# A third group of the first product as seven quarter products, with a new table of places

## The chip, the cores and the metric

The kernel runs on one core of a Trainium2 chip. The metric is the device time of one execution in microseconds; lower is better. The engines are named as in the profile: PE (TensorE, matrix products; PEld is its loading of weights), DVE (VectorE), ACT (ScalarE), POOL (GpSimd) and SP (SyncE); the last two only start transfers here, but for a tiny copy by which POOL waits.

## The reference

Eight batches of eight heads of normalised linear attention, then two matrix products with a leaky ReLU between them:

```python
kv = einsum('bhsd,bhse->bhde', k, v)            # 64 x 64 per head
o = einsum('bhsd,bhde->bhse', q, kv)            # 576 x 64 per head
x = o / sqrt(mean(o * o, -1) + 1e-6) * g_norm   # then 4608 tokens x 512
h = x @ w_in                                    # 4608 x 2048, "first product"
g = maximum(h, 0) + alpha * minimum(h, 0)
out = g @ w_out                                 # 4608 x 512, "second product"
```

Inputs and the output are float32. The kernel computes in float16 with float32 sums.

## The kernel before

The 4608 tokens are worked through in nine blocks (w = 0 to 8) of 512 tokens. A block needs the attention of its tokens (made while the block before it is in the products), the first product, and the second one, which runs into the next block. Blocks 0 and 1 are written out by hand. From block 2 on (line 1443 on) the work is a list of steps with a key, what it needs, and a function that records the instructions.

**The steps**, by the names that the text uses (block and number behind them):

- `M` (put_tile, L1513; m1_mm, L643): one of 16 tiles of 128 features of the first product, 4 matmuls of 128x512. The first of a block is parted in `Ma` (3 of 4 token tiles, L676) and the rest. `r` is ACT's ReLU of the negated tile (m1_neg, L652), `s` DVE's combine into g (m1_sum, L658).
- `f` (put_fast, L1464; m1_prod, L1254): the 16 tiles are four groups s = 0 to 3 of four tiles. A group can instead be made as a 2 x 2 block product by Strassen's scheme in Winograd's form: seven products of quarters, each 4 matmuls of 128x256. They stand in the order 1, 5, 6, 2, 7, 4, 3 of needs; products 1, 6, 7 and 4 add up in one PSUM bank Y. ACT copies that bank's state three times: `seed` (into bank X, L1270), `u2` and `u3` (L1273), and the next product may only add to Y when the copy is done: f6 after seed, f7 after u2, f4 after u3. DVE adds `c22` and `c12` (L1276), and ReLU (L1314) and combine (L1321) follow for the quarters 11, 12, 21, 22 (`r11`, `s11` and so on; a combine of a quarter is two instructions of 128x256).
- `t` (x_sum, L1233): four sums of quarters of x for these products, on DVE. `a` (a_sum, L1215): four sums of quarters of w_in for a group s, made once on DVE in block 2 and kept in a stage buffer of q, k or v that has become free.
- `p` (prod_mm, L862): a quarter of one of the seven products of the second product, 4 matmuls of 128x256, in the order 1, 2, 6, 7, 4, 5, 3 of products; its banks are read by the `y` steps (y_read, L929): `p1`, `seed`, `u2`, `u3`, `c11`, `c21` on ACT, `c22` and `c12` on DVE. `S` are its sums on DVE (s_pair, L806). `st` stores a quarter of the block's output (by POOL, `c12` by SP).
- `kv` and `kvc` (L1339, L1352): kv of a batch on PE, its copy on ACT. `R` (rows_mm, L508): the attention of two token tiles on PE; kv and the R steps of block 4 on use one PSUM buffer in turn. `q2`, `q3` (rows_sq, L584): squares and sums of a tile on ACT, 16 instructions; `rs` (L594) the reciprocal root on ACT; `n` (rows_norm, L610) the norm on DVE; `x` (x_move, L622) the transposing transfer into x, issued by SP.
- `ld` (put_load, L1705): a load of q, k or v, issued by POOL behind a copy of one element (gate, L1404) of the g that was recorded last; `q` (dma_t, L402): the transpose of a part of q, issued by SP.

**The order.** A table AT holds a number, a place, for each name. Prefixes of a name tell of block 2 (b), earlier (o), late ones (l) and block 8 (e); all other blocks share one entry, moved by 27.0 a block (LOOP). in_order takes, of the steps whose needs are recorded and whose buffer is to be had, the one with the smallest place:

```python
return (w - 2) * LOOP + AT[name], name
...
s = min((s for s in todo if usable(s)), key=lambda s: place(s[0])[0] + 1e-6 * rank[s[0]])
```

The order of recording is the order of each engine's queue. So the table decides what waits behind what on PE, ACT, DVE, POOL and SP; the steps from block 4 to block 7 stand in the same order in each block.

M1_FROM (L1200) says from which block on a group is made by quarter products; it is groups 2 and 3 from block 3 on. Four PSUM banks (h1, h2, m0, m1) go round among the tiles and the groups: a tile takes one, a group three (Y, V, X).

Of the kernel before, what the change touches and what calls it, by code (L numbers as in the profile page):

```python
# [17 lines left out]
def kernel(  # L18
# [1178 lines left out]
    h_turn[0] = 2  # L1197
    h_tags[0] = ("h1", "h0", "h2")

    M1_FROM = {2: 3, 3: 3}  # L1200
    HD = NC // 2
    spare, xsums, m1s = {}, {}, {}
    SPARE = {1: "q", 2: "k", 3: "v"}
# [556 lines left out]
    for w in range(1, NW):  # L1760
# [2 lines left out]

    LOOP = 27.0
    AT = {
# [67 lines left out]
    }  # L1833

    def place(key):

        what, w, *x = key
        if what == "f":
# [88 lines left out]
```

## Time and profile before

| | |
|---|---|
| median of 3 runs | 271.57 us (271.28 to 271.68) |
| the profiled execution | 271.5 us; span from first to last instruction 269.7 us |
| granted PE clock | 1.000 |
| transfers | 35.61 MB, mean 132 GB/s |
| PE, 128x512 of the first product (L643) | x348, 379 ns each |
| PE, 128x256 of the second product (L897) | x880, 273 ns each |
| PE, 128x256 of quarter products (L1254) | x336, 273 ns each |
| DVE, combine 128x512 (L658) | x96, 741 ns each |
| DVE, combine 128x256 (L1321) | x96, 474 to 479 ns each |
| ACT, ReLU of a tile (L652) | x96, 596 ns each |

The durations of one engine's instructions overlap: a matmul or a vector operation begins before the last one has ended. What an instruction costs its engine in a full queue is the time from its start to the next start, which the timeline of the engine gives. In the timeline a line holds a run of equal instructions: start, time until the last of them ended, engine, line, operation, what it writes from what, shapes, how many, and in brackets the idle time before it with what ended it.

### The profile page before, as it was taken

The page shows a single profiled execution, that of the slowest core. Times are in us where ns is not written, and L with a number is a line of the kernel's source. Part 1 is how long each engine was busy: PE and PEld are TensorE (multiplying, and loading weights), DVE is VectorE, ACT ScalarE, POOL GpSimd, SP SyncE. Part 2 cuts the span into 40 slices and gives each one's busy share as a digit, 9 for nine tenths or more (in the row PEclk, how much of TensorE's full clock was granted, in tenths as well). Part 3 has the DMA queues.
Part 4 walks back from the last instruction along what each step waited for, and adds up shares of the span by engine and source line. Part 5 has one row for each costly group of instructions (what it writes and reads, how often), then busy time and mean ns, then how long its engine had stood idle before and what let it go on. Part 6 is the DMA issues. An engine that isn't in the chain of part 4 may idle for free.

```text
span 269.7 us, 6668 instructions
## 1 busy us (share of the span) xinstructions
PE 262.0 (97%) x2430; PEld 182.4 (68%) x2430; DVE 225.8 (84%) x434; ACT 193.6 (72%) x686; POOL 94.6 (35%) x158
## 2 busy tenths in 40 slices
PE   7899999999999989999999999999999999999995
PEld 2454444456556756886688768876886688678884
DVE  7459727998987868988899889988998999978963
ACT  3567475786479789779977997799779974757410
POOL 8863453513530295470366043904130003001200
PEclk9999999999999999999999999999999999999999
DMA  7999999998998699999979989999664023100313
GB/s 151 193 201 202 197 197 193 174 197 113 173 188 122 77 136 169 171 183 145 148 88 165 191 115 85 122 192 144 93 123 113 1 41 118 41 0 2 131 66 118
DMA packets 91573, 35.61 MB, mean 132 GB/s; under 512 B 62980, under 2 KB 89748, under 8 KB 91540
## 3 DMA queue, kind: packets, MB, share of 16 engines
q0 software_dynamic: 57872, 23.83, 71.1%
q1 hardware_dynamic: 32628, 10.34, 22.4%
q10 hardware_dynamic: 1040, 1.02, 1.2%
q8 instruction: 19, 0.31, 0.5%
q14 instruction: 14, 0.11, 0.2%
HBM read 36.71 MB, written 9.44 MB: 171 GB/s over the span
## 4 chain that ended last, share of the span: by engine, by line
PE 76%; DMA 14%; ACT 4%; issue 2%; POOL 2%; DVE 1%; POOLq 0%; ACTq 0%
PE h_ps L643 20%; PE yY L897 15%; PE yX L897 9%; PE yZ L897 8%; PE mY L1254 8%; DMA w_out_sb<-in_moe_w_out_dram 5%; PE mV L1254 4%; DMA qst<-in_q_dram 4%; PE y L688 4%; DMA w_in_sb<-in_moe_w_in_dram 4%; ACT sq_sb L584 2%; PE h_ps L676 2%; PE mX L1254 2%; DMA qt_sb<-qst 2%; PE or_ps L521 1%
## 5 line engine op out<-in xcount | busy, mean ns | idle before, releaser
L643 PE MATMUL h_ps<-xt,w_in_sb 128*128 128x512 f16 x348 | 83.3, 379 | 0.0
L658 DVE SCALAR_TENSOR_TENSOR gt<-m_sb,beta_sb,h_ps 128x512 f16<-128x512 f32 x96 | 67.1, 741 | 4.7 <-ACT m_sb L652 4.0
L652 ACT ACTIVATE m_sb<-h_ps 128x512 f32<-128x512 f32 x96 | 54.7, 596 | 16.1 <-PE h_ps L643 12.9
L643 PEld LDWEIGHTS <-w_in_sb 128*128 128x128 f16 x348 | 33.0, 98 | 31.9 <-issue 0.4
L897 PEld LDWEIGHTS <-s 128*128 128x128 f16 x496 | 48.0, 98 | 8.7 <-DVE s L815 0.2
L897 PEld LDWEIGHTS <-gt 128*128 128x128 f16 x384 | 37.5, 98 | 8.2
L1404 POOL COPY gate_sb<-gt 1x1 f16<-1x1 f16 x39 | 11.9, 305 | 85.0 <-DVE gt L658 49.2
L584 ACT ACTIVATE sq_sb<-or_ps 128x64 f16<-128x64 f32 x192 | 39.6, 277 | 0.0
L584 ACT ACTIVATION_READ_ACCUMULATOR sq_sb<-or_ps 128x1 f32 x192 | 39.4, 264 | 0.0
L700 POOL DMA_DIRECT2D out_dram<-y_sb x32 | 20.5, 643 | 52.2 <-ACT y_sb L946 44.3
L897 PE MATMUL yX<-w_out_sb,gt 128*128 128x256 f16 x256 | 34.6, 273 | 0.0
L897 PE MATMUL yY<-wsum,s 128*128 128x256 f16 x256 | 32.3, 273 | 0.0
L610 DVE TENSOR_TENSOR x_rows<-or_ps,rstd_r 128x512 f16<-128x512 f32 x27 | 17.4, 686 | 11.4 <-ACT rstd_r L594 11.3
L1321 DVE SCALAR_TENSOR_TENSOR gt<-m_sb,beta_sb,mh 128x256 f16<-128x256 f32 x48 | 20.5, 479 | 1.3 <-ACT m_sb L1314 1.2
L1314 ACT ACTIVATE m_sb<-mh 128x512 f32<-128x512 f32 x24 | 15.1, 629 | 6.3 <-DVE mh L1276 6.3
L208 POOL DMA_DIRECT2D qst<-in_q_dram x20 | 17.9, 898 | 2.6 <-issue 2.2
L1273 ACT COPY mu<-mY 128x512 f32<-128x512 f32 x24 | 14.1, 589 | 4.9 <-PE mY L1254 4.4
L1276 DVE TENSOR_TENSOR mh<-mV,mu 128x512 f32<-128x512 f32 x24 | 16.4, 685 | 0.6 <-ACT mu L1273 0.4
L688 PE MATMUL y<-w_out_sb,gt 128*128 128x512 f16 x64 | 16.3, 379 | 0.4 <-DMA w_out_sb<-in_moe_w_out_dram 0.4
L897 PE MATMUL yZ<-wsum,s 128*128 128x256 f16 x120 | 16.2, 273 | 0.0
L897 PE MATMUL yY<-wsum,gt 128*128 128x256 f16 x128 | 15.4, 273 | 0.0
L1254 PEld LDWEIGHTS <-w_in_sb 128*128 128x128 f16 x144 | 14.1, 98 | 1.6
(147 smaller groups left out, 416.1 us busy)
## 6 DMA issues: line engine op xcount, KB each, us to landing
out_dram<-y_sb POOLq DMA_DIRECT2D x16, 256.0 KB, 3.2
kst<-in_k_dram POOLq DMA_DIRECT2D x7, 512.0 KB, 7.0
vst<-in_v_dram POOLq DMA_DIRECT2D x6, 512.0 KB, 8.8
qst<-in_q_dram POOLq DMA_DIRECT2D x20, 128.0 KB, 5.1
w_out_sb<-in_moe_w_out_dram POOLq DMA_DIRECT2D x8, 256.0 KB, 11.3
out_dram<-y_sb SPq DMA_DIRECT2D x5, 256.0 KB, 2.3
w_in_sb<-in_moe_w_in_dram POOLq DMA_DIRECT2D x2, 512.0 KB, 10.5
qst<-in_q_dram POOLq DMA_DIRECT2D x2, 512.0 KB, 12.3
```

The costliest lines, as they stand in the source:

```text
L208: nc.gpsimd.dma_start(out=stages[b, "q"][:, t, :, :], in_=srcs["q"][b, :, t * P : (t + 1) * P, :].rearrange("h p d -> p h d"),)
L584: nc.scalar.activation(out=sq[:, half, j], in_=o_ps[:, half, j], func=AF.Square, accum_out=ssq[:, half, j : j + 1],)
L610: nc.vector.tensor_tensor(out=xr[:].rearrange("p j h d -> p h j d"), in0=o_ps, in1=rstd[:].unsqueeze(3).to_broadcast([P, 2, NPAIR, D]), op ...
L643: nc.tensor.matmul(out=h_ps[:], lhsT=w_in_blk(c, g), rhs=xts[w][:, c, :], start=(c == 0), stop=(c == NC - 1),)
L652: nc.scalar.activation(out=neg[w, g][:], in_=h_ps[:], func=AF.Relu, scale=-1.0)
L658: nc.vector.scalar_tensor_tensor(out=gts[w, i][:, r, :], in0=neg.pop((w, g))[:], scalar=beta_sb[:, g : g + 1], in1=h_ps[:], op0=ALU.mult, ...
L688: nc.tensor.matmul(out=y[:], lhsT=gt_cols(w, g, a * P, (a + 1) * P), rhs=w_out_blk(g), start=(n == 1), stop=(n == NF),)
L700: engs[store_turn[0] % len(engs)].dma_start(out=dst, in_=src)
L897: nc.tensor.matmul(out=bank, lhsT=lhs, rhs=rhs, start=fresh, stop=(c == NK - 1), skip_group_check=True,)
L1254: nc.tensor.matmul(out=t[bank][:, r, :], lhsT=lhs[:, c, r * P : (r + 1) * P], rhs=rhs[:, c, :], start=(fresh and c == r == 0), stop=(c == ...
L1276: nc.vector.tensor_add(out=h_tile(t, what)[:, :, HW:W], in0=src[:], in1=u[:])
L1321: nc.vector.scalar_tensor_tensor(out=gts[w, i][:, r, cols], in0=m, scalar=beta_sb[:, g : g + 1], in1=h, op0=ALU.mult, op1=ALU.add,)
```

## The change

Two places of the kernel function change. Group s = 1 of the first product is made by seven quarter products from block 4 on, beside groups 2 and 3. So in blocks 4 to 8 four tiles M4 to M7 with their ReLUs and combines go, and the steps f11 to f17, seed, u2, u3, c22, c12 and the ReLUs and combines of four quarters come, and four sums a11 to a14 of w_in in block 2, kept in the second stage buffer of q. And all numbers of the table AT are new, with entries for the new steps, so that the order of every engine changes from block 2 on.

```diff
-    M1_FROM = {2: 3, 3: 3}
+    M1_FROM = {1: 4, 2: 3, 3: 3}
...
     LOOP = 27.0
     AT = {
-        "eyu3": -53629.57, "eyc21": -52723.24, "f2r11": -8398.49, "br7": -7586.48, "byu2": -7581.06,
...
+        "lkvc": -18398.72, "lq22": -18387.22, "lq23": -18384.30, "lq32": -18384.10, "r1": -18371.94,
...
+        "M0": 54.03, "M2": 54.03, "M1": 54.50, "M3": 54.81, "f11": 55.20, "bM12": 55.29, "ep23": 55.45,
...
+        "S30": 60.41, "f16": 60.63, "f21": 61.35, "M7": 61.86, "M5": 61.89, "f17": 62.03, "bM13": 62.09,
+        "f12": 62.19, "f15": 62.22, "f1s11": 62.90, "f14": 63.11, "f13": 63.25, "f1s22": 64.19, "f2c22": 64.26,
...
     }
```

The recorded order of PE for a whole block, before and after (block 5; a step with no block number belongs to it, and p4 is the second product of block 4):

```
before: M0 M2 p4:10 p4:11 M3 p4:12 p4:13 M1 kv6 M4 M6 R6:3 p4:60-63 p4:20 p4:21 f21 M5 M7 p4:70 f26 p4:71-73
        f27 f25 f22 f31 f24 f23 p4:40-43 p4:22 f36 p4:23 p4:50 p4:51 f37 f35 p4:52 p4:53 f34 R7:1 Ma6 f33 p4:30-33 f32
after:  Ma M0 M2 p4:13 M1 kv6 M3 f11 R6:3 p4:20-22 f16 p4:23 p4:60-63 f21 f17 f12 f15 p4:70 R7:1 f14 f13 p4:71-73
        p5:10 f26 f22 p5:11 f27 f25 p4:40 f31 f24 f23 p4:41-43 f35 f36 f32 p4:50 f37 p4:51-53 p5:12 f33 f34 p4:30-33
```

and of ACT from the ReLU of M3 to the third copy of group 1, after:

```
r3 seed(f1) q2(6:2) q2(6:3) q3(6:2) q3(6:3) rs(6:2) rs(6:3) u2(f1) c11(y4) u2(y4) u3(f1)
```

132 rows, old and new, of the table AT are left out of this document.

## The prediction

> **What bounds the kernel now.** I first read the page's parts 1 and 4, then the busy time by stretches of 20 us, then the starts of single instructions by engine.
>
> ```profile
> PE 262.0 (97%) x2430; PEld 182.4 (68%) x2430; DVE 225.8 (84%) x434; ACT 193.6 (72%) x686; POOL 94.6 (35%) x158
> PE 76%; DMA 14%; ACT 4%; issue 2%; POOL 2%; DVE 1%; POOLq 0%; ACTq 0%
> 120.00:140.00 20.00, 20.00 (x211) 14.89 (x210) 18.09 (x34) 18.47 (x91) 6.08 (x11) 1.00 0.91 134
> 180.00:200.00 20.00, 20.00 (x216) 15.55 (x214) 18.50 (x35) 16.14 (x58) 5.50 (x9) 1.00 0.83 130
> ```
>
> In the stretches (length, then busy time of PE, PEld, DVE, ACT, POOL, then the clock) PE is busy all of the time at clock 1.00, and DVE 18 to 18.5 of 20. Matmuls overlap, so busy alone does not prove that PE is full; the starts do:
>
> ```profile
> 66.60 1.04 PE L897 MATMUL yX<-w_out_sb,gt 128*128 128x256 f16 x8
> 68.23 0.81 PE L676 MATMUL h_ps<-xt,w_in_sb 128*128 128x384 f16 x4 [0.60 <-DVE gt L658]
> 94.15 0.60 PE L897 MATMUL yX<-w_out_sb,gt 128*128 128x256 f16 x4
> 95.47 0.38 PE L676 MATMUL h_ps<-xt,w_in_sb 128*128 128x128 f16 x4 [0.72 <-DMA xt<-x_rows]
> 157.12 1.92 PE L897 MATMUL yY<-wsum,s 128*128 128x256 f16 x16
> 158.88 1.04 PE L897 MATMUL yX<-w_out_sb,gt 128*128 128x256 f16 x8
> 159.75 0.60 PE L1254 MATMUL mY<-xt,w_in_sb 128*128 128x256 f16 x4
> 160.19 1.89 PE L643 MATMUL h_ps<-xt,w_in_sb 128*128 128x512 f16 x8
> 161.91 0.60 PE L897 MATMUL yY<-wsum,s 128*128 128x256 f16 x4
> ```
>
> From start to start, 16 matmuls of 256 columns take 1.76 us (109 ns each), a quarter group of four takes 0.44, and eight of 512 columns take 1.72 (216 each). At this pace a steady block is full: 0.88 for M0, 7 groups of 0.866, 14 + 28 quarter groups of 0.4375, 0.85 for kv and 2 x 0.43 for rows make 27.0 us, and the blocks do follow each other by 27.0 to 27.1 (the x16 group of 157.12 comes back at 184.24). **So Tensor is the bound from 68 us on**, but for gaps at these places: 68.23 is 0.76 after the eight yX should have ended (66.60 + 8 x 0.109), 95.47 is 0.88 late, rows of block 4 at 102.98 are 0.38 late, and six smaller ones of 0.06 to 0.15 sum to 0.6: 2.6 us in all.
>
> **The change, part by part.**
>
> *Tensor, -2.0 us.* In blocks 4 to 8 the group s=1 drops 16 matmuls of 512 columns (16 x 216 ns = 3.46) for 28 of 256 (28 x 109 = 3.06): -0.40 a block, -2.0 in five. The weight loads (98 ns each) fit under 109, as they do in the two groups done so today. A steady block would be 26.6.
>
> *Vector and Scalar, off the path if the cover holds.* The costs by start-to-start times:
>
> ```profile
> 162.86 1.40 DVE L658 SCALAR_TENSOR_TENSOR gt<-m_sb,beta_sb,h_ps 128x512 f16<-128x512 f32 x2
> 164.18 1.29 DVE L817 TENSOR_TENSOR s<-gt 128x1024 f16<-128x1024 f16 x2
> 167.16 0.68 DVE L1276 TENSOR_TENSOR mh<-mV,mu 128x512 f32<-128x512 f32 x1
> 167.76 0.86 DVE L1321 SCALAR_TENSOR_TENSOR gt<-m_sb,beta_sb,mY 128x256 f16<-128x256 f32 x2
> 168.54 0.68 DVE L819 TENSOR_TENSOR s<-gt,s 128x1024 f16<-128x1024 f16 x1
> ```
>
> A 512-wide combine costs 0.66, a pair of 256-wide ones 0.79, an add 0.60. The block drops 4 x 0.66 = 2.63 and gains 2 x 0.60 + 4 x 0.79 = 4.36: +1.7. Vector's block is then 4 x 0.66 + 3 x 4.36 + 4 t sums of 0.335 + 8 pair sums of 0.605 + 2 y adds and 4 norms of 0.60 = 25.5 us (23.8 before) of Tensor's 26.6. It fits, if Vector waits for less than 1.1 us in a block; today it waits 27.0 - 23.8 = 3.2, with no cost. Scalar drops 4 ReLUs of 0.49 and gains 3 copies of 0.48 and 4 ReLUs of 0.48 to 0.53: +1.5, to some 23.3 of 26.6. The four weight sums of s=1 (4 x 0.335 = 1.3) fall once into block 2, where DVE stands idle 2.5 us in one wait (for rstd_r at 82.35).
>
> The Trainium skill, "VectorE: DVE Perf Modes", section "The DRAIN you can't avoid", says that the next Vector operation does not start until the pipe is empty. By that each instruction would cost its whole duration. This trace shows otherwise: combines of 740 ns start 658 ns apart. The sum above goes by the starts.
>
> *What becomes late next: the wait that I expect.* I laid the new order of each engine end to end by these paces. In blocks 4 to 7 Tensor runs M3, then f11, rows (the next block's second pair), three groups of p2, f16, one of p2, four of p6, f21, and then f17. f17 adds to the bank that Scalar must first copy as u2. Between them Scalar has: the ReLU of M3, the seed, 32 square instructions for those rows, two rstd, then u2. The trace shows what this run costs:
>
> ```profile
> 157.38 0.22 ACT L584 ACTIVATE sq_sb<-or_ps 128x64 f16<-128x64 f32 x1
> ...
> 160.80 0.49 ACT L594 ACTIVATE rstd_r<-ssq_r,eps_t 128x8 f32<-128x8 f32 x2
> 161.20 0.56 ACT L938 COPY u<-yY 128x512 f32<-128x512 f32 x1
> ```
>
> From first square to the next copy 3.82. So from M3's end: 0.20 until Scalar may start (a matmul lasts 379 against its pace of 216, and 0.04 for the signal) + 0.49 + 0.48 + 3.82 + 0.59 + 0.03 = 5.61. Tensor's own work there is 11 quarter groups and rows, 4.81 + 0.43 = 5.24. **Tensor waits 0.37, in four blocks.** A second ring has nearly the same length: f33 ends, Vector does c12, t2, s22, n, s21, n, s12, y c12 (5.1), Scalar seed, ReLU, kvc, ReLU, seed, squares, u2 (7.2), Tensor f17 to f33 (14.4), and 0.3 for three handovers: 27.0. Both say that the new block is 27.0 to 27.1, not 26.6: what s=1 gains in blocks 4 to 7 is eaten. I take 0.42 a block, +1.7. It is not under 0 (Tensor can't be ahead of its own order), and not over 0.9 unless Vector falls behind.
>
> *Block 8* has no rows to square, so f17 is free there. Its end is tighter: S10 and S20 now stand on Vector ahead of the y c22 that p3 of block 7 waits for (about 0.4), and three waits of under 0.1 follow. +0.6, from 0 to 1.
>
> *The start, blocks 2 and 3.* kv of block 3 and a half p2 group now stand ahead of the first products, and fill the 0.76 hole; M2 and M3 come before Ma, whose transposed rows have long been issued (62.84). The loads of q for block 4 are issued when Vector is at s8 and s11 of block 2 (about 85.5 to 89.5) instead of 91.65 to 97, and all five transposes of q3 go out together, so rows of block 4 find their q. Against that, thirteen short sums on Vector stand ahead of the first combine: p6 waits 0.2, M7 0.1, M6 0.1; the norms of rows 3 and 2 are asked for in the order in which the later comes first, so M9 and p5 wait 0.2 and 0.35, and f27 of block 3 0.2. +1.2. The last transpose of x for block 3 goes out at about 92.0 (90.92 before). It then took 4.5 us to land, which would be just in time for the last part of M0 at 96.4. Rows of this tile in the trace give 2.4 to 7.1 us to land, so the price is 0 to 2.6; I take 0, as the q loads that shared its time have moved ahead of it.
>
> *Sum.* -2.0 - 2.6 + 1.2 + 1.7 + 0.6 = **-1.1 us**. The profiled execution took 271.5 us (span 269.7, and 1.8 around it), the median of the runs is 271.57, so the two agree. **270.4 us.**
>
> **The rivals.**
> - *Tensor stays full (268.6).* The four waits at f17 and the block 8 waits vanish because Scalar gets through the squares before I think: -2.0 - 2.6 + 1.2 + 0.5. For it: today's order has no wait in steady blocks. Against: 3.82 is measured, and the order gives it 5.24 at most. Chance 0.17.
> - *The ring is longer (271.5).* 0.2 to 0.3 more a block, since several handovers in my walk have under 0.1 of slack (f27 waits for u2, rows for kvc). Then all is eaten. Chance 0.18.
> - *Vector becomes the bound (274, slower).* It has 1.1 us of slack a block where it waits 3.2 now. If 2.2 of these waits stay, the block is 25.5 + 2.2 = 27.7, 0.6 over my 27.1, in five blocks +3.0, and with all 3.2 the block is 28.7 and the time 278. It decides from 1.6 us of waits on (25.5 + 1.6 = 27.1). For it: DVE at 90% and more in every stretch. Against: laid end to end, its waits come to 1.5. Chance 0.12.
> - *A transfer lands late at the start (273.0, slower).* The 2.6 us above, with x at 7.1. In the trace one wait for x and one for q show that this place is close. Chance 0.08.
> - *Vector's instructions do not overlap (283).* By whole durations the block is 4 x 0.741 + 3 x 5.18 + 1.68 + 5.50 + 1.36 + 2.74 = 29.8, 2.8 more than today's, in four to five blocks +11 to +14. Against: the same sum gives 27.6 for today, longer than the 27.0 that the trace shows. Chance 0.01. This is what the rule of the Trainium skill quoted above would make of it.
> - That the third group is not made is excluded: the built order has its 28 matmuls in each of five blocks.
>
> **How the numbers follow.** My forecast keeps 0.44. About 0.2%, 0.54 us, is what a measurement of this kernel can tell from none. Forecast (0.36 of its 0.44 below 271.0) and full Tensor (0.17), with 0.05 of the longer ring, give 0.58 faster; the rest of the ring and of the forecast 0.21 same; Vector, transfers and overlap 0.21 slower. The likeliest case alone spans 269.5 to 271.3. With the full Tensor below and the ring and part of the slower cases above, 8 in 10 lie in 268.6 to 272.5.
>
> **What would show it.** The profile of the changed kernel should show mY matmuls at L1254 waiting for a mu copy (L1273), some 0.4 us once in each of blocks 4 to 7 and not in block 8; blocks 27.0 to 27.1 apart; no gap at 68; DVE near 95% in the steady stretches, never the reason of more than 0.1 us of Tensor's waits. Wrong: blocks 26.6 apart (full Tensor), or over 27.3 with Tensor waiting for Vector (the Vector rival), or a gap over 1 us before 105 us with a DMA as its reason.

## The result, and the profile after

The changed kernel is slower: 273.02 us (median of 20 runs, 271.52 to 276.56) against 272.05 us of the kernel before in the same comparison (20 runs, 271.02 to 276.0); the ratio is 1.0038, with a 95% interval of 1.0021 to 1.0055. Ratios and intervals, here and below, leave out executions more than 1.5% above the fastest of their kernel; medians hold all. A gain of 1.1 us was forecast, a loss of 1.0 us came, and 273.02 lies outside the range of 268.6 to 272.5. The profiled executions lie closer together: 271.94 us (span 270.0) against 271.5 (269.7). So the changed kernel's profile is one of its quick executions, 1.1 below its median, and that of before lies 0.5 below its own. The fastest of the 20 runs, 271.52 and 271.02, are 0.5 apart as well. Both differences have to be explained: why the profiles differ by +0.4 and not by -1.1, and why the medians differ by more than the profiles.

The lines of the page that answer to the first ones of before, busy time and shares of the chain that ended last:

```profile
PE 262.4 (97%) x2490; PEld 188.3 (70%) x2490; DVE 232.7 (86%) x468; ACT 200.0 (74%) x701; POOL 95.9 (36%) x158
PE 53%; DMA 16%; DVE 12%; ACT 12%; issue 4%; POOL 1%; SPq 1%; DVEq 0%; ACTq 0%; POOLq 0%
```

Two stretches of 20 us of the same kernel (length, then busy time of PE, PEld, DVE, ACT, POOL, the clock, DMA share, GB/s):

```profile
120.00:140.00 20.00, 19.90 (x233) 15.71 (x231) 18.92 (x38) 17.50 (x76) 11.92 (x22) 1.00 1.56 151
180.00:200.00 20.00, 19.89 (x240) 16.71 (x240) 18.77 (x38) 18.72 (x79) 1.43 (x2) 1.00 0.44 82
```

PE has 60 matmuls more and the same busy time, and its share of the chain fell from 76% to 53%: DVE and ACT now each carry 12% of what sets the end. In the stretches PE is no longer busy throughout. PE's timeline in block 4 shows the place (start, duration, what):

```profile
130.62 1.91 PE L897 MATMUL yY<-wsum,s 128*128 128x256 f16 x16
132.37 0.60 PE L1254 MATMUL mY<-xt,w_in_sb 128*128 128x256 f16 x4
133.07 0.60 PE L1254 MATMUL mY<-t,qst 128*128 128x256 f16 x4
133.50 0.60 PE L1254 MATMUL mX<-xt,w_in_sb 128*128 128x256 f16 x4
```

ACT's timeline at the same time:

```profile
131.93 0.61 ACT L594 ACTIVATE rstd_r<-ssq_r,eps_t 128x8 f32<-128x8 f32 x2
132.41 0.61 ACT L1273 COPY mu<-mY 128x512 f32<-128x512 f32 x1
```

f21 starts at 132.37, f17 at 133.07, 0.70 later where 0.44 is the pace: f17 waits 0.26 for the copy u2 that started at 132.41, behind the squares and the two rstd. The same wait is 0.38, 0.27 and 0.41 in blocks 5 to 7. The blocks follow each other by 27.15 (kv at 125.81, 152.96, 180.11).

At the start the hole at 68 us is filled (kv stands at 67.77, right behind the eight yX), and others have come (PE's timeline; in brackets the idle time ahead and what ended it):

```profile
72.58 1.05 PE L897 MATMUL yY<-wsum,s 128*128 128x256 f16 x8 [0.20 <-DVE s L831]
...
92.18 1.91 PE L897 MATMUL yZ<-wsum,s 128*128 128x256 f16 x16 [0.18 <-ACT y_sb L946]
...
97.08 0.38 PE L676 MATMUL h_ps<-xt,w_in_sb 128*128 128x128 f16 x4 [0.16 <-DMA xt<-x_rows]
```

Counted against the pace, the waits from 62 us on are 2.6 us in the trace of before and 4.6 in that of after: 1.7 at the start (up to f27 of block 3), 1.3 at f17, 0.7 at f27 of blocks 4 to 7, 0.85 in block 8 and at the two f13 that wait for c22, at 216 and 241 us (0.44 of it at 254 us, for y c22). From the first kv of block 2 to the last matmul it is 213.2 us before and 213.3 after: the 2.0 us of work that went are just filled by 2.0 us more of waits. Of the 0.3 us between the two spans 0.2 lies ahead of this kv (53.74 and 53.55 us), where the two orders are the same.

The page's part on transfers, of the kernel before (what, queue, count, at loads the KB of each, median us from issue to landing):

```profile
vst<-in_v_dram POOLq DMA_DIRECT2D x6, 512.0 KB, 8.8
xt<-x_rows SPq DMA_TRANSPOSE x27, 3.4
qt_sb<-qst SPq DMA_TRANSPOSE x20, 4.0
```

The same of the changed kernel:

```profile
vst<-in_v_dram POOLq DMA_DIRECT2D x6, 512.0 KB, 10.8
xt<-x_rows SPq DMA_TRANSPOSE x27, 4.9
qt_sb<-qst SPq DMA_TRANSPOSE x20, 7.0
```

Nothing was added to what is moved (35.61 MB before, 35.60 after), and yet these land later, and so do the loads of k (7.0 to 8.6) and POOL's stores (3.2 to 4.1); the small loads of q (5.1 to 5.2) and the weights do not. The new table asks for the rows of the block after next some 10 us earlier in a block (R6:1 behind p3:70 instead of ahead of Ma5: 9.1 us after kv instead of 18.9). So in block 4 the loads of q (issued from 125.99 to 133.02) go out just ahead of those of k and v (134.26 and 137.80), and four transposes of q (136.31 to 142.52) while these are under way.

### The profile page after: what moved, and what is told of

Its sections match the earlier page's. It is cut to its first block, busy times and chain, and to the rows that moved or that the text cites. A ratio compares the mean times of both kernels' runs of the same rounds, so it can differ in the third digit from the quotient of the medians.

```text
span 270.0 us, 6813 instructions
## 1 busy us (share of the span) xinstructions
PE 262.4 (97%) x2490; PEld 188.3 (70%) x2490; DVE 232.7 (86%) x468; ACT 200.0 (74%) x701; POOL 95.9 (36%) x158
## 2 busy tenths in 40 slices
DMA packets 91572, 35.60 MB, mean 132 GB/s; under 512 B 62980, under 2 KB 89748, under 8 KB 91540
## 4 chain that ended last, share of the span: by engine, by line
PE 53%; DMA 16%; DVE 12%; ACT 12%; issue 4%; POOL 1%; SPq 1%; DVEq 0%; ACTq 0%; POOLq 0%
PE h_ps L643 11%; PE yY L897 10%; PE mY L1254 8%; ACT sq_sb L584 6%; PE yX L897 5%; DMA w_out_sb<-in_moe_w_out_dram 5%; PE yZ L897 4%; DVE gt L1321 4%; PE y L688 4%; PE mV L1254 4%; DMA qt_sb<-qst 3%; DMA w_in_sb<-in_moe_w_in_dram 3%; DMA qst<-in_q_dram 3%; PE mX L1254 2%; DVE mh L1276 2%
## 5 line engine op out<-in xcount | busy, mean ns | idle before, releaser
L643 PE MATMUL h_ps<-xt,w_in_sb 128*128 128x512 f16 x268 | 64.9, 379 | 0.1
L652 ACT ACTIVATE m_sb<-h_ps 128x512 f32<-128x512 f32 x76 | 43.9, 598 | 21.5 <-PE h_ps L643 11.8
L658 DVE SCALAR_TENSOR_TENSOR gt<-m_sb,beta_sb,h_ps 128x512 f16<-128x512 f32 x76 | 54.0, 741 | 4.0 <-ACT m_sb L652 3.3
L897 PEld LDWEIGHTS <-s 128*128 128x128 f16 x496 | 48.1, 98 | 8.6 <-DVE s L831 1.1
L897 PEld LDWEIGHTS <-gt 128*128 128x128 f16 x384 | 37.1, 98 | 7.6
L643 PEld LDWEIGHTS <-w_in_sb 128*128 128x128 f16 x268 | 25.2, 98 | 23.9 <-issue 0.4
L897 PE MATMUL yX<-w_out_sb,gt 128*128 128x256 f16 x256 | 35.7, 273 | 0.0
L897 PE MATMUL yY<-wsum,s 128*128 128x256 f16 x256 | 32.2, 273 | 0.2 <-DVE s L831 0.2
L1321 DVE SCALAR_TENSOR_TENSOR gt<-m_sb,beta_sb,mh 128x256 f16<-128x256 f32 x68 | 29.2, 478 | 0.4 <-ACT m_sb L1314 0.4
L1404 POOL COPY gate_sb<-gt 1x1 f16<-1x1 f16 x39 | 13.5, 345 | 39.3 <-DVE gt L658 29.1
L1276 DVE TENSOR_TENSOR mh<-mV,mu 128x512 f32<-128x512 f32 x34 | 23.3, 686 | 4.5 <-PE mV L1254 4.2
L1314 ACT ACTIVATE m_sb<-mh 128x512 f32<-128x512 f32 x34 | 22.0, 646 | 4.9 <-DVE mh L1276 4.9
L1273 ACT COPY mu<-mY 128x512 f32<-128x512 f32 x34 | 20.5, 604 | 3.5 <-PE mY L1254 3.4
L1254 PEld LDWEIGHTS <-w_in_sb 128*128 128x128 f16 x204 | 19.7, 98 | 3.5
L897 PE MATMUL yY<-wsum,gt 128*128 128x256 f16 x128 | 16.6, 273 | 0.0
L897 PE MATMUL yZ<-wsum,s 128*128 128x256 f16 x120 | 16.2, 272 | 0.2 <-ACT y_sb L946 0.2
## 6 DMA issues: line engine op xcount, KB each, us to landing
vst<-in_v_dram POOLq DMA_DIRECT2D x6, 512.0 KB, 10.8
```

The lines of the kernel that those rows point to most:

```text
L643: nc.tensor.matmul(out=h_ps[:], lhsT=w_in_blk(c, g), rhs=xts[w][:, c, :], start=(c == 0), stop=(c == NC - 1),)
L652: nc.scalar.activation(out=neg[w, g][:], in_=h_ps[:], func=AF.Relu, scale=-1.0)
L658: nc.vector.scalar_tensor_tensor(out=gts[w, i][:, r, :], in0=neg.pop((w, g))[:], scalar=beta_sb[:, g : g + 1], in1=h_ps[:], op0=ALU.mult, ...
L897: nc.tensor.matmul(out=bank, lhsT=lhs, rhs=rhs, start=fresh, stop=(c == NK - 1), skip_group_check=True,)
L1254: nc.tensor.matmul(out=t[bank][:, r, :], lhsT=lhs[:, c, r * P : (r + 1) * P], rhs=rhs[:, c, :], start=(fresh and c == r == 0), stop=(c == ...
L1273: nc.scalar.copy(out=t[what][:], in_=t["Y"][:])
```

## The experiments

Theory A: the order of the new table has waits that stand in every execution (f17 above all). Theory B: its transfers land later, in some executions too late. Each kernel was timed beside the kernel before on the same chip; ratios are to that. The kernel before had medians of 271.75 (first four kernels), 271.42 (next four), 271.54 (next four), 272.03 (the four that leave work out) and 271.71 us (last two).

### The change once more, and the table alone

```diff
-    M1_FROM = {1: 4, 2: 3, 3: 3}
+    M1_FROM = {2: 3, 3: 3}
```

e0_again is the changed kernel as it is; the edit is that of e1_table.

> The changed kernel unaltered, once more. Theory A (the order's own waits): its trace has the same waits at the same places as the first (f17 0.27 to 0.41 in blocks 4 to 7, f27 0.17, the last y c22 0.44, about 1.5 us before 100 us), blocks 27.15 apart, and its median lies 0.7 to 1.3 us over that of the kernel before. Theory B (loads that sometimes land late): a second profile shows one or two waits of over 0.5 us for transposed rows of x or q before 110 us that the first does not show, and the span differs from the first's 270.0 by that amount.

> The new table with the third group left as eight ReLU products: the table alone. Theory A (the group's waits are what was lost, the table is a gain): no f17 waits, blocks of 27.0, the start without the 2.6 us of gaps but with its 1.2 to 1.7 of small waits, 0.5 at the end: 0.3 to 0.9 us under the kernel before. Rival (the table itself costs: loads moved, and the order of the norms): 0.5 to 1.5 us over the kernel before, and the changed kernel no slower than this one.

Measured: the change again 272.57 us, 1.0031 (1.0004 to 1.0058); the table alone 271.93, 1.0011 (0.9987 to 1.0035). So the slowdown repeats. The table without the group is within the noise of the kernel before; its blocks are 27.1 and 27.0 and it has no f17 wait, which is theory A's half. It was not the gain that A had hoped for either: the last two x of block 3 made PE wait 0.97 in its profile.

The second profile of the changed kernel fell on an execution of 275.87 us, the longest of its 12; it serves only to see which waits can grow, and explains no median. f17, f27 and y c22 wait as before, within 0.15 us. What grew are waits for transfers: 1.7 for the last two x of block 3 (0.3 in the first profile), 0.9 and 0.6 at kv, 1.0 behind the sums t of block 6. Parts of its chain from 140 us on (start, duration, what):

```profile
140.75 14.96 DMA vst<-in_v_dram
155.71 0.14 issue
155.84 0.82 PE kv_ps L1344 x40
...
164.86 11.32 DMA xt<-x_rows
176.18 0.03 issue
```

A load of v took 15.0 us and a transpose of x 11.3. DVE stood at the first t of block 6 until the x was there and everything behind it was late, PE by way of mh. In the quick execution the last of these x had landed at 171.52 and was asked for at 172.29, 0.8 us later; in the kernel before it had landed at 170.98 and was first needed at 173.27 (Ma6 on PE), 2.3 us later.

### Taking the waits away one by one, by places

```diff
 # e3_u2: second square of row tiles 2 and 3 behind u2 of the new group
+        if what == "q3" and x[0] in (2, 3) and w >= 5:
+            return (w - 2) * LOOP + 33.70, name
 # e13_f17: f17 behind f12 and f15
-        "f17": 62.03
+        "f17": 62.25
 # e11_t: t1, t3, t2 behind y c12
-        "t1": 42.42, "t3": 40.14, "t2": 50.64
+        "t1": 53.40, "t3": 53.45, "t2": 53.50
 # e5_tail: S10, S20 of block 8 behind y c22
-        "eS10": 39.14, "eS20": 40.81
+        "eS10": 74.60, "eS20": 74.80
 # e6_loads: all "ld" places of blocks 5 to 7 from the old table
 # e12_all: e6, e13, e11, e5, y c12 ahead of the last norm and of s12, n2 ahead of n3 in block 2
```

> The changed kernel, with the second square of each of the last two tiles of rows moved behind the copy u2 of the new group, so that 16 to 24 fewer square instructions stand ahead of it. Theory A (f17 waits for Scalar's squares, and nothing is late behind it): the four waits at f17 go, blocks come 26.8 to 26.9 apart, 1.1 to 1.4 us under the changed kernel. Rival (the second ring through Vector's sums, y c12, and Scalar's seed is as long): the f17 wait goes but as much appears at kv, f27 or rows; blocks stay 27.0 to 27.2, 0 to 0.4 us under the changed kernel.

> The changed kernel with f17 on Tensor behind f12 and f15 instead of ahead of them: 0.88 us more of Tensor's own work between M3 and f17, against the wait of 0.27 to 0.41. Theory A: the four waits at f17 go, the ring through Vector loses 0.88 as well, blocks come 26.7 to 26.8 apart, 1.2 to 1.5 us under the changed kernel. Rival (u3 comes half a microsecond later, and with it c22, the combines and f27): as much is waited for at f27 or f14, 0 to 0.4 us under it.

> The changed kernel with three of the next block's short sums t on Vector behind y c12, instead of ahead of the combines of the last group, some 7 us later; Tensor's and Scalar's orders as they are. Theory B (Vector reaches these sums before the transposes of x have landed in some executions, and everything behind them is late): no wait of Vector for x behind 110 us, median 0.3 to 0.8 us under the changed kernel's. Theory A: they cost nothing where they are, but a shorter Vector ring (y c12 comes 1.0 us earlier) may take 0.1 a block, 0 to 0.4 us in all.

> The changed kernel, with the sums S10 and S20 of block 8 on Vector behind y c22 of block 7 instead of ahead of it. Theory A: the wait of 0.44 us at 254 us goes and nothing replaces it, 0.4 us under the changed kernel. Rival: S20 is late for its own product and the same 0.4 comes back within 10 us: 0 to 0.1 us under the changed kernel.

> The changed kernel with the places of the loads of k, v and q for blocks 5 to 7 taken from the old table; the orders of Tensor, Vector and Scalar are the changed kernel's. Theory B (the new table sends these loads out in one bunch ahead of and beside the transposes of x, which land later for it): the median landing of the x transposes falls from 4.9 us towards 3.4 to 4, the waits for x on Vector and Tensor behind 110 us go, the median falls 0.3 to 0.8 us under the changed kernel's. Theory A (only the order's own waits): no more than 0.2 us.

> All the mends at once on the changed kernel: old places for the loads of blocks 5 to 7, f17 behind f12 and f15, the three sums t and the last norm of the first pair behind y c12, the norm of row tile 2 ahead of that of 3 in block 2, S10 and S20 of block 8 behind y c22. If the waits found in the traces are the cause and they add up (f17 1.3, tail 0.4, late x 0.5 to 1, start 0.3): 2.3 to 3 us under the changed kernel, 1.3 to 2 under the kernel before. Rival (a wait that is removed comes back as another, since the rings have no slack): under 1 us below the changed kernel.

| kernel | median us | ratio (95%) |
|---|---|---|
| e3_u2 | 282.72 | 1.0374 (1.0332 to 1.0415) |
| e13_f17 | 275.22 | 1.0119 (1.0085 to 1.0153) |
| e11_t | 272.79 | 1.0037 (1.0006 to 1.0068) |
| e5_tail | 272.62 | 1.0034 (1.0016 to 1.0052) |
| e6_loads | 274.02 | 1.0075 (1.0048 to 1.0103) |
| e12_all | 277.05 | 1.0197 (1.0174 to 1.0221) |

None helped, and each shows what was late next.

*e3_u2*: f17 is on time, and the block is 28 to 33 us. ACT's timeline:

```profile
133.12 0.22 ACT L584 ACTIVATE sq_sb<-or_ps 128x64 f16<-128x64 f32 x1 [0.76 <-DVE x_rows L610]
```

The moved square of tile 2 waits for DVE's norm of tile 3: both read the same PSUM buffer, and a square recorded behind a norm of the pair waits for it. The Trainium skill ("PSUM — Partial Sum Buffer", "PSUM bank collisions raise a hardware error") says that two engines must not be in one bank of the same partitions at once, reads against reads included, and that the compiler's back end adds a dependency between them; a wait of 0.76 us between two reads agrees with such an order, while no run here shows what a collision does. Then the norm of tile 2 holds DVE, x goes out at 138.07 instead of 133.70 (SP now has two transposes of q ahead of it, issued from 133.37 on), and PE stands 2.6 to 2.8 us at 151. A further 1.1 to 1.6 us in each of blocks 4 to 7 is waited for ACT's copy u of the second product, which stands behind the moved square. Neither theory's numbers had this.

*e13_f17*: the rival was right. f17 starts on time (134.96), and f13, f26 and f27 wait instead (in blocks 7 and 8 f14 too, 0.54 and 0.40). PE's timeline:

```profile
136.27 0.61 PE L1254 MATMUL mY<-t,w_in_sb 128*128 128x256 f16 x4
136.96 0.60 PE L1254 MATMUL mV<-xt,qst 128*128 128x256 f16 x4
...
138.70 0.60 PE L897 MATMUL yX<-w_out_sb,gt 128*128 128x256 f16 x4
139.41 0.60 PE L1254 MATMUL mY<-t,kst 128*128 128x256 f16 x4
139.85 0.60 PE L1254 MATMUL mX<-xt,w_in_sb 128*128 128x256 f16 x4
140.28 0.60 PE L897 MATMUL yX<-w_out_sb,gt 128*128 128x256 f16 x4
140.93 0.27 PE L1254 MATMUL mY<-t,kst 128*128 128x256 f16 x1
```

Steps of 0.69, 0.71 and 0.65 where 0.44 is the pace: 0.7 in a block for 0.3 saved, blocks of 27.5.

*e5_tail*: again the rival. yZ starts on time at 254.49, and 0.58 is waited for S20 at 259.43. *e11_t*: no wait for x on DVE, but other things ended up late in its profile (1.1 at kv for a load of v, 0.7 at f11 of block 7 for a combine that now stands behind the sums). *e6_loads*: theory B's mechanism is right and its mend wrong. With the loads at their old places the transposes of x land in 3.7 us and those of q in 4.4, nearly as in the kernel before, but the new order needs the rows early: R6:1, due 0.44 after the line above it, comes after 1.53, so it waits 1.1 for q (PE's timeline):

```profile
133.97 0.60 PE L897 MATMUL yY<-wsum,s 128*128 128x256 f16 x4
135.50 0.41 PE L521 MATMUL or_ps<-kv_masked,qt_sb 64*128 64x64 f16 x16 [0.93 <-DMA qt_sb<-qst]
```

*e12_all* adds these up (1.9 at R6:1, 1.8 at S20). One of its parts worked: with n2 ahead of n3 the wait for the last x of block 3 is gone.

### Whole tables made by the paces, and the old one with the new transfers

> Three groups, as in the changed kernel, on another table of places. Its orders, laid end to end at the start-to-start paces of the traces, have no wait of Tensor over 0.2 us between the first products of block 2 and block 8, also when every transfer lands 2 us later than in the traces so far: f17 stands behind enough products, the last norms and the loads go out earlier. Theory (the third group's 0.40 a block is real, and what ate it are the rings of the table and its tight transfers): blocks 26.6 apart, 1.4 to 2.2 us under the kernel before, 2.2 to 3 under the changed one. Rival (three groups leave Scalar and Vector so little room that waits come back that the paces do not show, or earlier loads crowd the transfers again): blocks 26.9 or more, at best 0.7 under the kernel before.

> A second table of this kind for three groups, found independently, with other orders on every engine. The same numbers as for the first: blocks 26.6 apart and 1.4 to 2.2 us under the kernel before by the theory, at best 0.7 under it by the rival. If the two tables differ by over 0.7 us, it is the transfers, which differ most between them, and not the group.

> Two groups, as in the kernel before, on a table made with the same care: blocks of 27.0, nothing waited for between block 2 and 8. By the theory 0.4 to 0.9 us under the kernel before, and the three groups of the other two kernels 1.3 to 1.6 under this one: that is the group's own worth in five blocks, 2.0, less the longer tail. Rival: as fast as the three groups within 0.5 us.

> The kernel before, two groups and its old table, with only the places of the loads of k, v and q and of the transposes of q for blocks 5 to 7 taken from the new table. Theory B (the new table's transfers are bunched and land later, by themselves): transposes of x land in 4 us and more instead of 3.4, those of q in 6 to 7 instead of 4.0, and the time rises by 0.3 to 1.0 us or spreads more. Rival (only the new order of rows makes them matter): landing times rise, the time stays within 0.2 us.

Here the edit is the table AT. In e14_three, e14b_three and e15_two all its numbers are new, so that no short diff tells anything; in e9_bunch the ld and q entries of blocks 5 to 7 in the kernel before are those of the changed one, such as

```diff
-        "ldq2-6": 9.13, "ldv4-7": 11.01, "ldq3-6": 27.66, "q1-5": -72.29
+        "ldq2-6": -0.01, "ldv4-7": 0.04, "ldq3-6": -0.01, "q1-5": -218.83
```

Measured: 284.23 us, 1.0458 (1.0421 to 1.0495); 284.07, 1.0442 (1.0406 to 1.0479); 274.66, 1.0119 (1.0074 to 1.0164); 288.18, 1.0610 (1.0576 to 1.0643). No gain came. For the two tables with three groups the rival alone, waits that the paces do not show, describes what happened; the other two expectations missed on both sides.

In the two tables for three groups the blocks are 28 to 29 us: the orders put squares behind a norm of their pair, as in e3_u2, a rule that the paces did not hold: ACT's squares wait 11.1 and 11.7 us in all for norms. In e14b_three the second product (L897) waits 1.1 to 2.1 us in each of blocks 4 to 7 for ACT's copy u (L938), which stands behind such squares. e15_two has blocks of 26.2, 29.6 and 28.1, with 2.3 us at 150 us for mh and 1.8 at 83 us for a q. e9_bunch did not measure what bunching costs: SP works its queue in order, and x came to stand behind transposes of q. Rows of block 4 that DVE had normalised by 109.2 went out at 117.24 and 124.96, behind two and four such transposes, the first of which stood for a load that landed at 114.45. This place cost 10.6 us (PE's timeline):

```profile
130.30 1.44 PE L676 MATMUL h_ps<-xt,w_in_sb 128*128 128x384 f16 x4 [10.59 <-DMA xt<-x_rows]
```

Its landing times say something all the same: q in 7.1 and v in 10.7 us, as in the changed kernel, but x in 3.4, as before. With e6_loads, the places of the loads and of q's transposes account for the late q; that they alone make x late is not shown.

### Leaving work out, orders as they are

```diff
 # e16_sq, e19: second half of the squares of row tiles 2 and 3, w >= 5
-        for j in range(NPAIR):
+        if w >= 5 and half and i in (2, 3):
+            nc.scalar.copy(out=ssq[:, half, :], in_=o_ps[:, half, :, 0])
+        for j in range(NPAIR if not (w >= 5 and half and i in (2, 3)) else 0):
...
 # e17, e18, e19: stores of blocks 1 to 7, 8 of 128 partitions each
-        engs[store_turn[0] % len(engs)].dma_start(out=dst, in_=src)
+        few = slice(0, 8) if short[0] else slice(None)
+        engs[store_turn[0] % len(engs)].dma_start(out=dst[few], in_=src[few])
...
```

> The changed kernel, all orders as they are, with 14 of the 32 square instructions ahead of u2 left out in blocks 4 to 7 (the second half of two row tiles' squares is replaced by one copy each; these rows are scaled wrongly). It takes some 1.4 us of Scalar's time ahead of u2, and no place is moved. Theory A (the f17 wait, worked out as 0.37 and seen as 0.27 to 0.41, is what eats the group's gain in these blocks): the waits at f17 go, blocks come 26.7 to 26.8 apart, 1.2 to 1.6 us under the changed kernel. Theory B (transfers decide): blocks shorter in the profile, but the median at most 0.5 us under the changed kernel's, since earlier products only wait longer for x, k and v.

> The kernel before, with the stores of its results of blocks 1 to 7 cut to 8 of 128 partitions (the rest of the output is not written): some 8 MB less to move. It is the partner of the next kernel. Theory B (transfers cost little here, since landing x takes 3.4 us as it is): 0 to 0.5 us under the kernel before.

> The changed kernel with the same short stores. Theory B (some 0.7 of the 1.0 us comes from transfers that land late): landing of the x transposes falls from 4.9 towards 4, and the time lies within 0.4 us of the partner's, 1 us and more under the changed kernel. Theory A (the order's own waits): it stays 0.7 to 1.2 us over the partner.

> The changed kernel with both: fewer squares and short stores (both leave work out, as in the two kernels before). If the two causes are all there is, the third group's gain shows at last: 1.2 to 2 us under the kernel before with short stores. If it stays within 0.5 us of it, a third cause is left.

| kernel | median us | ratio (95%) | block 2's kv to last matmul, in the profile |
|---|---|---|---|
| e16_sq | 272.80 | 1.0016 (0.9991 to 1.0040) | 212.4 |
| e17_before_st | 271.47 | 0.9984 (0.9968 to 0.9999) | 213.4 |
| e18_after_st | 272.01 | 0.9999 (0.9981 to 1.0017) | 213.1 |
| e19_after_sq_st | 271.54 | 0.9978 (0.9951 to 1.0005) | 212.0 |

Without the squares f17 goes on at pace (132.49, 132.93, 133.37 on PE), and blocks are 26.9 and 26.8. So the f17 wait is what theory A says, and nothing as long stands behind it in the profile. The median follows by 0.6 (1.0038 to 1.0016) where the four waits were 1.3: between what A and B expected, and the two intervals overlap. With short stores, 6.8 MB less, the transposes of x land in 2.7 us (4.9 with full stores; those of q still in 7.2) and the wait for the last x of block 3 is gone; changed and old kernel are then 0.15% apart, 0.4 us, instead of 0.3 to 0.4%. The intervals overlap, so this points to B and does not prove it.

e19_after_sq_st, which has both, came out level with its partner e17_before_st (271.54 and 271.47 us, ratios 0.06% apart), where 1.2 to 2 us under it were expected if the two causes were all. So a third part is left, as that expectation says. Its trace shows what it can be: waits of the order that neither edit touches are still there, about 1.5 at the start, 0.6 at f27 in blocks 3 to 6 and 0.9 for c22 from 214 us on.

### An order that keeps the rule, and the changed kernel's transfers

> Three groups, with every load, store and transpose in the changed kernel's order, and the orders of Tensor, Scalar and Vector made anew by the start-to-start paces of the traces, this time with the rule that the runs showed: a square of a pair of row tiles and a norm of the same pair wait for each other, so all four squares stand ahead of both norms. Tensor has 0.44 more work ahead of f17 and the half-norms of the start come earlier. Theory (the group's gain was lost to the order alone): blocks 26.7, the wait at 254 us gone, 1.5 to 2.3 us under the changed kernel, 0.5 to 1.3 under the kernel before. Rival (with Tensor full at 26.7 the transfers, asked for 0.45 a block earlier, are late instead): blocks over 26.9 or waits for x, k and v of over 1 us, within 0.5 us of the changed kernel.

> Two groups with the same care and the same order of transfers: blocks 27.0, nothing else waited for. By the theory 0.3 to 1.0 us under the kernel before and 0.3 to 0.7 us over the three groups; by the rival as fast as the three groups or faster.

The edit is again the whole table (and, for e21_two, M1_FROM as in e1_table). In a steady block the orders that differ are, changed kernel first:

```text
PE   p4:30-33 Ma6 M6:0 M6:2 p5:13 ... f6:16 p5:23 p5:60-63 f6:21 f6:17 f6:12 f6:15 p5:70
PE   Ma6 M6:0 p4:30-33 M6:2 p5:13 ... f6:16 p5:23 p5:60-63 f6:15 f6:21 f6:17 f6:12 p5:70
ACT  q2(2) q2(3) q3(2) q3(3) rs rs u2 y:c11 y:u2 u3 r11 r22 q2(0) r21 seed r12
ACT  q2(3) q3(3) q2(2) q3(2) rs rs u2 y:u2 u3 r11 y:c11 q2(0) r22 seed r12 r21
```

Measured: three groups 270.05 us, 0.9954 (0.9933 to 0.9976); two groups 275.38, 1.0046 (1.0010 to 1.0082), from 271.4 to 280.5. By the ratios the three groups are 1.25 us under the kernel before and some 2.2 under the changed one: faster than both, as the theory had it. The shares of its chain, from its page:

```profile
PE 69%; DVE 11%; DMA 11%; ACT 5%; issue 2%; POOL 1%; POOLq 0%
```

Two stretches of it, as above:

```profile
120.00:140.00 20.00, 20.00 (x237) 16.17 (x236) 19.34 (x38) 17.69 (x77) 11.97 (x22) 1.00 1.32 144
180.00:200.00 20.00, 20.00 (x216) 17.54 (x214) 19.18 (x40) 19.38 (x93) 1.43 (x2) 1.00 0.33 71
```

Its PE at f17:

```profile
130.92 0.60 PE L1254 MATMUL mV<-t,qst 128*128 128x256 f16 x4
131.36 0.60 PE L1254 MATMUL mY<-xt,w_in_sb 128*128 128x256 f16 x4
131.80 0.60 PE L1254 MATMUL mY<-t,qst 128*128 128x256 f16 x4
132.23 0.60 PE L1254 MATMUL mX<-xt,w_in_sb 128*128 128x256 f16 x4
```

f15, f21, f17, f12 follow at 0.44: no wait. kv comes at 124.37, 151.30, 178.02, 26.9 and 26.7 apart, and from block 2's kv to the last matmul it takes 211.2 us. In these two stretches DVE is busy 19.2 to 19.3 of 20 and PE waits for nothing of it; elsewhere PE does wait for DVE, at most 0.52 us (at 213.63). The norms of tiles 3 and 2 of block 3 start at 87.9 instead of 89.7, and the last x of block 3 goes out 2.4 us earlier, so nothing is waited for at 96. The landing times are about those of the changed kernel (x 4.4, q 7.2), and from 62 us on no wait of PE for a transfer is left in this profile: late transfers did no harm once the order left them room. The two groups are as fast as the kernel before in the profile (271.84) but not in most runs; which wait grows there is open, so this pair does not tell what the third group alone is worth.

## Why the prediction was wrong

The mechanism of the steady blocks was right. Two steps failed: the last transpose of x at the start, "I take 0", and the handovers with "under 0.1 of slack", which were priced at nothing in the sum. The terms one by one:

- *Tensor, -2.0*: right. With the waits gone the blocks are 26.7 (e20_three), as 26.6 was worked out.
- *Waits of before, -2.6*: the hole at 68 us and the wait for q at 102.98 went, that for x did not (0.88 before, 0.32 in the changed kernel's profile, more in others).
- *The start, +1.2*: mis-sized. Found are 1.7: p6 0.37 (0.2 taken), M9 0.27, p5 0.24 (0.35 taken), f27 0.12, three of about 0.1 at the M and p tiles, 0.15 at 63 us, and x 0.32. The step that failed is the last one: "I take 0, as the q loads that shared its time have moved ahead of it". These loads did go out earlier (86.64 to 89.61). But the last x, issued at 92.30, let PE go on only 4.8 us later (4.5 before), and the three ahead of it landed in 4.9 to 7.1 us (2.4 to 3.4 before). Its own range, 0 to 2.6, holds what was seen. In the eight profiles of kernels with this start and full stores, that of e0_again left aside, PE waits for it 0.33, 0.58, 0.59, 0.72, 0.97, 1.07, 1.26 and 1.32 us, in the middle 0.85; the changed kernel's own is the smallest.
- *f17, +1.7*: place and cause right, size 1.3 (0.26 to 0.41 a wait for 0.37 and 0.42); e16_sq takes it away with the squares. But "several handovers in my walk have under 0.1 of slack" was the rival's remark: f27 waits 0.17 to 0.20 for its u2 in each block, 0.7 in all, beside f17's 1.3. Together 2.0. That the blocks still come 27.15 apart, so close to the 27.0 to 27.1 forecast, is luck: f17 waits less than taken, and f27 was not in the sum.
- *Block 8, +0.6*: y c22 0.44 as forecast; with the waits for c22 ahead of it 0.85.
- *The sum*: -2.0 - 2.6 + 4.6 is 0.0 and not -1.1. All the terms that were too small are waits behind a new neighbour in some queue, by 0.1 to 0.5.
- *"The two agree"*, of profile and median: true of the kernel before, not of a new order. The changed kernel's profile was near its best case: by the eight profiles a usual execution waits some 0.5 us more for the last x of block 3 alone, as much as separates the two medians beyond the two profiles. In the kernel before this wait was 0.88, and 0.34 in e9_bunch, which has its orders there. So the last 0.5 to 0.6 us is put down to transfers whose landing rose from 3.4 to 4.9 and from 4.0 to 7.0 us, the x of block 3 first; e18_after_st, which takes that wait away, brings the kernels to 0.15%. This is argued: the timed executions were not profiled, and e19_after_sq_st shows that the waits of the order still cost time without it.
- *Rivals*: the longer ring (271.5) had the place of f27 right and came nearest to the profile (271.94). Vector never was the bound (19.3 of 20 busy in the quickest kernel), though it makes PE wait 0.3 to 0.4 at p6 and M9 of block 2. The rule of the Trainium skill quoted above ("VectorE: DVE Perf Modes", "The DRAIN you can't avoid") would have made it so, with blocks of 29.8; blocks of 26.7 with all three groups disagree with that sentence of it. They agree with another one of the same section, which the prediction left out: an operation that is not held starts earlier. The late transfer at the start, given 0.08, was part of the story, at about a third of its price of 2.6, and in the second profile of the changed kernel it has brothers at 128, 156 and 178 us that were not priced at all.

## What to carry to other kernels

Where the bound engine has no slack, price a new order by its queues: walk each ring of handovers, and give every new pair of neighbours 0.1 to 0.2 us, not 0. A wait that is moved away came back at the next copy of the same ring (e13_f17, e5_tail); what helped in e20_three was an order in which the bound engine has 0.44 us more of its own work ahead of f17 and ACT's copies for f26 and f27 come 0.4 us earlier behind kv (10.98 and 12.50 for 11.36 and 12.86). Read the landing times of the transfers of both kernels beside the waits: if they rise, the profiled execution may be a lucky one, and more profiles of kernels with the same start tell how lucky.

## What the runs showed of the hardware

- A square on ACT recorded behind a norm on DVE of the same PSUM buffer waits for it (0.76 us in e3_u2, 1.33 in e14b_three), though both only read; in e20_three, with the squares ahead of both norms, none of these waits is left.
- The same bytes in another order of issue land later: medians of x 3.4 and 4.9 us, q 4.0 and 7.0, v 8.8 and 10.8. With the old places of the loads they are 3.7, 4.4 and 8.7 (e6_loads). A load of v took 15.0 and an x 11.3 in one long execution. With 6.8 MB less of stores x lands in 2.7, q still in 7.2 (e18_after_st).
- SP worked its queue in order: rows of x ready at 109.2 went out at 117.24 and 124.96, behind transposes of q of which the first stood for its load until 114.45, and PE waited 10.6 us (e9_bunch).
- DVE was busy 97% of a stretch (19.34 of 20) in which PE waited for nothing of it (e20_three).
